# Sliding-window attention feeding a token mixer on one core: the token matrix reassociated away, and the score matmuls of two heads interleaved

## The chip, the cores and the metric

The kernel runs on one core of one Trainium2 chip. The metric is device time in microseconds, from start to end of one execution. The profile's span (first to last instruction) is about 2 us shorter. PE is the matrix engine, DVE the vector engine, ACT the scalar engine, POOL the engine that issues the loads. All ratios below are computed as the mean time of one kernel's fast runs over the mean of the fast runs of the other kernel in the same rounds, so they are not quite the ratios of the medians that are quoted.

## The reference, cut to what matters

```python
# q, k, v: (8 batches, 8 heads, 576 positions, 64)
scores = where(0 <= i-j < 128, q @ k.T / 8 - slope[h] * |i-j|, -1e9)
attn   = softmax(scores) @ v                       # per batch and head
x      = attn.transpose(0, 2, 1, 3).reshape(8, 576, 512)
# token mixing, per batch; w_q and w_k are (512, 64)
wq = x @ w_q                                       # 576 x 64
wk = x @ w_k                                       # 576 x 64
W_tok = wq @ wk.T / 8                              # 576 x 576, nothing nonlinear on it
mixed = W_tok @ x                                  # 576 x 512
out   = relu(mixed) @ w_out
```

## The kernel before: the parts that the change and the argument touch

The program is unrolled. The attention of batch b and the token mixing of batch b-1 are cut into chunks and laid down alternately; a scheduler then orders each engine's instructions. Two PSUM buffers of 1,024 fp32 columns (`pscore`) hold scores, four buffers of up to 512 (`ppool`) serve everything else.

```python
        def mk_qk(h):                       # scores of one head, five key blocks
            def f():
                ...
                ps = pscore.tile([P, 1024], FP32, name=f"ps{h}", tag="ps")
                for kb in range(NKB):
                    o, w = KB_OFF[kb], KB_WID[kb]
                    nc.tensor.matmul(ps[:, o : o + w],
                        kT[hb : hb + 64, hp, 128 * kb : 128 * kb + 128],   # 64 rows
                        qT[hb : hb + 64, hp, 128 * kb : 128 * kb + w], start=True, stop=True)
                pt = spool.tile([P, 1024], F16, name=f"pt{h}", tag="pt", bufs=8)
                nc.scalar.activation(out=pt, in_=ps, func=AF.Exp, scale=SCALE)
                nc.vector.tensor_tensor(out=pt, in0=pt, in1=bfull[h], op=ALU.mult)
...
        def mk_wtok(tcn):                   # 128 rows of the token matrix
            def f():
                ...
                nc.tensor.matmul(pw, lt, wqkT[0][:, 0:512], start=True, stop=True)
                nc.tensor.matmul(pwl, lt, wqkT[0][:, 512:576], start=True, stop=True)
                cp(nc.vector, dst[:n, 0:512], pw[:n])
                cp(nc.vector, dst[:n, 512:], pwl[:n])
...
        def mk_mixed(db):                   # 128 of 512 channels of the mixed result
            def f():
                ...
                for tcn in range(NQT):      # five contraction tiles, each a pair of matmuls
                    nc.tensor.matmul(pm, lt, st_["wtok"][tcn][:n, 0:512], ...)
                    nc.tensor.matmul(pml, lt, st_["wtok"][tcn][:n, 512:], ...)
                nc.scalar.activation(out=rm[:, db, 0:512], in_=pm, func=AF.Relu, scale=WSCALE)
                nc.scalar.activation(out=rm[:, db, 512:], in_=pml, func=AF.Relu, scale=WSCALE)
...
        chunks = [[mk_wq(0)], [mk_wtok(0), mk_wtok(1), mk_wtok(2)], [mk_wtok(3), mk_wtok(4)]]
        for db in range(4):
            chunks.append([mk_mixed(db)])
        for st in range(NQT):
            chunks.append([mk_out(st)])
```

The softmax here doesn't subtract the row's maximum and nothing guards it: scores larger than these inputs give would overflow.

## Time and profile before

The median is 270.46 us (270.09 to 270.84, two runs); the profiled run has a span of 267.9 us. I cut the span by events that can be found on the engine timelines. A period begins with a batch's first transposing matmul (tile `ptr`). Its part A ends where the batch's first exponential starts on ACT, part B ends with the eighth bias multiplication on DVE, part C ends where the next period begins. The last period ends with the first projection matmul (tile `pw`) of the last batch. What lies ahead of batch 1's period is the start, what follows the last period is the tail.

| before, us | start | A | B | C | period (mean of 7) | tail |
|---|---|---|---|---|---|---|
| length | 36.3 | 6.01 | 12.55 | 11.32 | 29.89 | 22.4 |
| of it at half clock | all | 0.7 | 4.9 | 0.5 | 6.1 | 8.1 |

The first two fences are from the profile page of before: the busy table, and the row of the 40-slice table that has the PE clock granted, in tenths.

```profile
PE 227.3 (85%) x2000; PEld 130.1 (49%) x2000; DVE 164.4 (61%) x426; ACT 128.9 (48%) x234; POOL 108.2 (40%) x134
...
PEclk9999999799968999879979997799959998899689
```

No engine is full, and the clock dips once in every period. The clock records begin at 41.4 us; ahead of that the row prints full clock because there is no record. There 128-column matmuls follow each other after 0.107 us, against 0.056 us at recorded full clock, so I count the start as half clock; the 0.7 us in A is the first part of batch 1's period. The mean clocks that the profile gives (0.915 here) count the start as full.

This is the stretch view of before for batch 4: parts A, B and C. The columns are the stretch, its length, then busy us of each engine with instruction counts, the granted clock, and DMA.

```profile
core 0: us, PE busy (x) PEld busy (x) DVE busy (x) ACT busy (x) POOL busy (x), PEclk, DMA share, GB/s
128.20:133.90 5.70, 5.00 (x62) 3.57 (x61) 3.16 (x7) 3.90 (x10) 5.70 (x8) 1.00 1.90 177
133.90:146.50 12.60, 10.28 (x77) 5.30 (x76) 8.38 (x20) 10.20 (x17) 5.14 (x7) 0.86 1.45 93
146.50:157.60 11.10, 10.89 (x116) 6.50 (x115) 8.83 (x28) 0.85 (x3) 1.71 (x2) 1.00 0.20 73
```

In part B, ACT is the engine with the most to do, but it is not back to back. This is the ACT timeline of before in that part; a bracket gives idle time just before the instruction and who ended it.

```profile
136.77 1.02 ACT L153 ACTIVATE pt_1975<-ps_1969 128x1024 f16<-128x1024 f32 x1
137.97 1.02 ACT L153 ACTIVATE pt_1999<-ps_1993 128x1024 f16<-128x1024 f32 x1 [0.18 <-PE ps_1993 L146]
...
140.81 0.60 ACT L270 ACTIVATE rm<-pm 128x512 f16<-128x512 f32 x1 [1.68 <-PE pml L268]
141.31 0.22 ACT L271 ACTIVATE rm<-pml 128x64 f16<-128x64 f32 x1
141.41 1.03 ACT L153 ACTIVATE pt_2008<-ps_2002 128x1024 f16<-128x1024 f32 x1
```

Between the fifth and the sixth exponential ACT stands 1.68 us for the first mixing pass. The PE and DVE timelines of before:

```profile
138.83 0.61 PE L266 MATMUL pm<-wtok_1914,x_1629 128*128 128x512 f16 x1
139.24 0.26 PE L268 MATMUL pml<-wtok_1914,x_1629 128*128 128x64 f16 x1
139.31 0.61 PE L266 MATMUL pm<-wtok_1921,x_1669 128*128 128x512 f16 x1
...
140.99 0.38 PE L266 MATMUL pm<-wtok_1914,x_1629 128*128 128x512 f16 x1
```

```profile
133.33 0.69 DVE L51 CAST wtok_1907<-pwt 128x512 f16<-128x512 f32 x1
133.94 0.21 DVE L51 CAST wtok_1907<-pwtl 128x64 f16<-128x64 f32 x1
134.07 0.68 DVE L51 CAST wtok_1914<-pwt 128x512 f16<-128x512 f32 x1
134.67 0.21 DVE L51 CAST wtok_1914<-pwtl 128x64 f16<-128x64 f32 x1
134.80 0.68 DVE L51 CAST wtok_1921<-pwt 128x512 f16<-128x512 f32 x1
```

From 136.9 to 140.4 the clock records say half clock, and a mixing pair takes 0.48 us from start to start (138.83 to 139.31) against 0.25 us at full clock. The records of matmuls overlap (0.38 us long, 0.25 us from pair to pair), so distances between starts are what adds up.

### The profile page before, as it was taken

What the parts mean: (1) busy time and instruction counts of PE and PEld (TensorE: products, weight loads), DVE (VectorE), ACT (ScalarE), POOL (GpSimd) and SP (SyncE); (2) the same over time, 40 slices, a digit from 0 to 9 for tenths busy, and PEclk for the clock granted to TensorE, in tenths of its full rate; (3) what the DMA queues carried; (4) which work ended last, traced back from release to release, by engine and by line L of the source; (5) the groups of instructions that cost most, each with busy time, mean ns of one, the idle gap of its engine ahead of it and who ended that gap; (6) DMA issues with size and microseconds to landing.
All of it is one profiled execution on the core that took longest, in us unless ns stands there. A gap on an engine that the chain in (4) does not pass through costs nothing.

```text
span 267.9 us, 5117 instructions
## 1 busy us (share of the span) xinstructions
PE 227.3 (85%) x2000; PEld 130.1 (49%) x2000; DVE 164.4 (61%) x426; ACT 128.9 (48%) x234; POOL 108.2 (40%) x134
## 2 busy tenths in 40 slices
PE   0477798989899997979888997989899998998894
PEld 0244665445544654445644655455544654454331
DVE  1134837578674858368594858477674869485504
ACT  3977218640767139540577128640767048711130
POOL 9999859402960079001970079102950000000000
PEclk9999999799968999879979997799959998899689
DMA  4999999903990299903992289903990220013005
GB/s 30 111 140 133 155 100 134 114 4 118 170 152 4 81 134 159 72 1 120 152 155 19 81 120 164 80 0 125 177 145 1 87 92 2 0 46 123 11 1 177
DMA packets 120425, 24.72 MB, mean 92 GB/s; under 512 B 115280, under 2 KB 115792, under 8 KB 120400
## 3 DMA queue, kind: packets, MB, share of 16 engines
q0 software_dynamic: 115152, 14.95, 86.9%
q1 hardware_dynamic: 5248, 9.44, 9.8%
q8 instruction: 15, 0.25, 0.4%
q14 instruction: 10, 0.08, 0.1%
HBM read 29.88 MB, written 9.44 MB: 147 GB/s over the span
## 4 chain that ended last, share of the span: by engine, by line
PE 35%; ACT 16%; issue 16%; DMA 13%; POOL 11%; DVE 8%; POOLq 0%; ACTq 0%
PE pm L266 12%; PE po L281 7%; DMA vnat<-in_v_dram 5%; PE px L180 4%; ACT rm L270 3%; POOL vnat L116 3%; DMA knat_433<-in_k_dram 3%; DVE osb L51 2%; DMA knat_3179<-in_k_dram 2%; DMA knat_126<-in_k_dram 2%; PE pml L268 1%; DMA qnat_886<-in_q_dram 1%; PE pxt L199 1%; ACT qT L49 1%; PE ptr L133 1%
## 5 line engine op out<-in xcount | busy, mean ns | idle before, releaser
L116 POOL DMA_DIRECT2D vnat<-in_v_dram x40 | 34.4, 884 | 85.6 <-issue 66.6
L49 ACT COPY qT<-ptr 128x512 f16<-128x512 f16 (+1 forms) x24 | 12.5, 521 | 70.5 <-PE ptr L133 70.3
L281 PE MATMUL po<-wout_sb,rm 128*128 128x512 f16 x160 | 41.2, 384 | 1.0
L51 DVE COPY osb<-po 128x512 f32<-128x512 f32 (+1 forms) x40 | 27.5, 688 | 12.9 <-PE po L281 11.9
L270 ACT ACTIVATE rm<-pm 128x512 f16<-128x512 f32 x32 | 19.6, 614 | 32.0 <-PE pml L268 32.0
L146 PEld LDWEIGHTS <-kT 64*128 64x128 f16 x320 | 25.2, 103 | 17.2 <-issue 9.2
L183 DVE RECIPROCAL invr<-px 128x4 f32<-128x4 f32 (+1 forms) x80 | 12.5, 171 | 17.1 <-PE px L180 17.0
L51 DVE COPY kT<-ptr 128x512 f16<-128x512 f16 (+1 forms) x24 | 9.1, 380 | 21.5 <-PE ptr L133 21.3
L281 PEld LDWEIGHTS <-rm 128*128 128x128 f16 x160 | 14.4, 99 | 14.2 <-issue 3.5
L51 DVE COPY xT<-pxt 128x512 f16<-128x512 f16 (+1 forms) x40 | 15.5, 388 | 0.7 <-PE pxt L199 0.5
L49 ACT COPY kT<-ptr 128x512 f16<-128x512 f16 x16 | 9.4, 588 | 3.8 <-PE ptr L133 3.8
L51 DVE COPY qT<-ptr 128x512 f16<-128x512 f16 x16 | 6.7, 421 | 5.2 <-PE ptr L133 5.2
L229 PE MATMUL pw<-xT,wqk_sb 128*128 128x512 f16 x32 | 9.9, 410 | 0.0
L271 ACT ACTIVATE rm<-pml 128x64 f16<-128x64 f32 x32 | 7.3, 230 | 0.0
L231 PE MATMUL pwl<-xT,wqk_sb 128*128 128x64 f16 x32 | 6.3, 201 | 0.0
L49 ACT CAST wqkT_3636<-pw 64x512 f16<-64x512 f32 x1 | 0.6, 580 | 10.2 <-PE pwl L231 10.2
L133 PE MATMUL ptr<-identh,qnat_108 128*128 128x128 f16 x4 | 0.6, 308 | 5.7 <-DMA qnat_108<-in_q_dram 5.7
L54 ACT ACTIVATE vnat<-identh 128x45 f16<-128x45 f16 x8 | 3.3, 412 | 3.5 <-DMA vnat<-in_v_dram 3.3
L229 PEld LDWEIGHTS <-wqk_sb 128*128 128x128 f16 x32 | 3.3, 104 | 3.3 <-issue 0.8
L249 PE MATMUL pwt<-wqkT_3636,wqkT_3637 64*128 64x512 f16 x5 | 2.2, 460 | 2.3 <-ACT wqkT_3637 L49 1.3
L54 ACT ACTIVATE kT<-bfull_88 128x256 f16<-128x256 f16 x8 | 3.6, 453 | 0.0
L231 PEld LDWEIGHTS <-wqk_sb 128*128 128x128 f16 x32 | 3.2, 103 | 0.2
(1015 smaller groups left out, 717.3 us busy)
## 6 DMA issues: line engine op xcount, KB each, us to landing
out_dram<-osb SPq DMA_DIRECT2D x32, 256.0 KB, 2.0
vnat<-in_v_dram POOLq DMA_DIRECT2D x32, 128.0 KB, 5.1
out_dram<-osb SPq DMA_DIRECT2D x8, 128.0 KB, 4.0
vnat<-in_v_dram POOLq DMA_DIRECT2D x8, 64.0 KB, 4.8
wout_sb<-in_moe_w_out_dram POOLq DMA_DIRECT2D x1, 512.0 KB, 6.4
qnat_108<-in_q_dram POOLq DMA_DIRECT2D x1, 128.0 KB, 3.5
knat_110<-in_k_dram POOLq DMA_DIRECT2D x1, 128.0 KB, 3.4
qnat_112<-in_q_dram POOLq DMA_DIRECT2D x1, 128.0 KB, 3.3
```

The lines of the kernel that those rows point to most:

```text
L49: eng.copy(out_ap, in_ap)
L51: eng.tensor_copy(out=out_ap, in_=in_ap)
L116: nc.gpsimd.dma_start(out=vnat[:n, kt, 0:H, 1:65], in_=v[b, :, ss, :].transpose([1, 0, 2]))
L146: nc.tensor.matmul(ps[:, o : o + w], kT[hb : hb + 64, hp, 128 * kb : 128 * kb + 128], qT[hb : hb + 64, hp, 128 * kb : 128 * kb + w], start ...
L180: nc.tensor.matmul(px[:, hh, :], lt, rt, start=(i == 0), stop=(i == len(mms) - 1))
L183: nc.vector.reciprocal(out=invr[:n], in_=px[:n, :, 0])
L229: nc.tensor.matmul(pw, wqk_sb[:, dc, :], xT[:, dc, 0:512], start=(dc == 0), stop=(dc == 3))
L231: nc.tensor.matmul(pwl, wqk_sb[:, dc, :], xT[:, dc, 512:576], start=(dc == 0), stop=(dc == 3))
L266: nc.tensor.matmul(pm, lt, st_["wtok"][tcn][:n, 0:512], start=(tcn == 0), stop=(tcn == 4))
L270: nc.scalar.activation(out=rm[:, db, 0:512], in_=pm, func=AF.Relu, scale=WSCALE)
L271: nc.scalar.activation(out=rm[:, db, 512:], in_=pml, func=AF.Relu, scale=WSCALE)
L281: nc.tensor.matmul(po, rm[:, db, lo : lo + 128], wout_sb[:, db, :], start=(db == 0), stop=(db == 3))
```

## The change

The intent: (wq wk^T) x equals wq (wk^T x). The product in brackets, G, is 64 x 512 and takes five matmuls; the 576 x 576 matrix, its ten copies out of PSUM per batch, and 16 of 20 pairs of mixing matmuls go away. wk is now needed with positions on rows, which takes 20 narrow matmuls. The second idea: the heads of a pair lie on rows 0 to 63 and 64 to 127, so their score matmuls are issued alternately, meant to run side by side.

```diff
-        def mk_qk(h):
+        def mk_qk2(hp):
...
+                pss = [pscore.tile([P, 1024], FP32, name=f"ps{hp}_{i}", tag="ps") for i in range(2)]
                 for kb in range(NKB):
                     o, w = KB_OFF[kb], KB_WID[kb]
-                    nc.tensor.matmul(ps[:, o : o + w], kT[hb : hb + 64, ...], qT[hb : hb + 64, ...])
+                    for i in range(2):
+                        hb = 64 * i
+                        nc.tensor.matmul(pss[i][:, o : o + w], kT[hb : hb + 64, ...], qT[hb : hb + 64, ...])
...
-        def mk_wtok(tcn): ...                       # five token tiles, ten copies
+        def wk():                                   # wk with positions on rows
+            for t in range(NQT):
+                for dc in range(4):
+                    nc.tensor.matmul(pk[:n, t, :], xT[:, dc, 128 * t : 128 * t + n],
+                                     wqk_sb[:, dc, 64:128], start=(dc == 0), stop=(dc == 3))
+            cp(nc.vector, wkn[:, 0:4, :], pk[:, 0:4, :])
+            cp(nc.vector, wkn[:64, 4, :], pk[:64, 4, :])
+        def gmat():                                 # G = wk^T x, 64 x 512
+            for t in range(NQT):
+                nc.tensor.matmul(pg[0:64], st_["wkn"][:n, t, :], ast["xs"][t][:n, :], ...)
+            cp(nc.scalar, g, pg[0:64])
         def mk_mixed(db):
-                for tcn in range(NQT): ...          # five pairs of matmuls
+                lt = st_["g"][:, 128 * db : 128 * db + 128]        # 64 rows
+                nc.tensor.matmul(pm, lt, st_["wqT"][:, 0:512], start=True, stop=True)
+                nc.tensor.matmul(pml, lt, st_["wqT"][:, 512:576], start=True, stop=True)
```

Cut from the diff: two fewer weight loads, two fewer copies and one fewer zero fill on ACT in the projection, and second buffers for `rm`, `wqT` and the new tiles.

More of the change, by code (lines that the diff above doesn't have):

```diff
@@ L87 @@
     wqk_sb = cpool.tile([P, 4, 128], F16, name="wqk_sb")
-    wkq_sb = cpool.tile([P, 4, 128], F16, name="wkq_sb")
     wout_sb = cpool.tile([P, 4, DM], F16, name="wout_sb")
     def load_weights():
-        for src, dsts in ((moe_w_q, (wqk_sb[:, :, 0:64], wkq_sb[:, :, 64:128])),
-                          (moe_w_k, (wqk_sb[:, :, 64:128], wkq_sb[:, :, 0:64]))):
-            for dst in dsts:
-                nc.gpsimd.dma_start(out=dst, in_=src.rearrange("(c p) j -> p c j", p=P))
+        for src, dst in ((moe_w_q, wqk_sb[:, :, 0:64]), (moe_w_k, wqk_sb[:, :, 64:128])):
+            nc.gpsimd.dma_start(out=dst, in_=src.rearrange("(c p) j -> p c j", p=P))
         nc.gpsimd.dma_start(out=wout_sb, in_=moe_w_out.rearrange("(c p) j -> p c j", p=P))
@@ L136, in mk_xpose @@
             return f
-        def mk_qk(h):
+        def mk_qk2(hp):
             def f():
                 qT, kT = st_["qT"], st_["kT"]
-                hp = h // 2
-                hb = (h % 2) * 64
-                ps = pscore.tile([P, 1024], FP32, name=f"ps{h}", tag="ps")
+                pss = [pscore.tile([P, 1024], FP32, name=f"ps{hp}_{i}", tag="ps") for i in range(2)]
                 for kb in range(NKB):
                     o, w = KB_OFF[kb], KB_WID[kb]
-                    nc.tensor.matmul(
-                        ps[:, o : o + w],
-                        kT[hb : hb + 64, hp, 128 * kb : 128 * kb + 128],
-                        qT[hb : hb + 64, hp, 128 * kb : 128 * kb + w],
-                        start=True, stop=True,
-                    )
-                pt = spool.tile([P, 1024], F16, name=f"pt{h}", tag="pt", bufs=8)
-                nc.scalar.activation(out=pt, in_=ps, func=AF.Exp, scale=SCALE)
-                nc.vector.tensor_tensor(out=pt, in0=pt, in1=bfull[h], op=ALU.mult)
-                st_.setdefault("pts", {})[h] = pt
+                    for i in range(2):
+                        hb = 64 * i
+                        nc.tensor.matmul(
+                            pss[i][:, o : o + w],
+                            kT[hb : hb + 64, hp, 128 * kb : 128 * kb + 128],
+                            qT[hb : hb + 64, hp, 128 * kb : 128 * kb + w],
+                            start=True, stop=True,
+                        )
+                for i in range(2):
+                    h = 2 * hp + i
+                    pt = spool.tile([P, 1024], F16, name=f"pt{h}", tag="pt", bufs=8)
+                    nc.scalar.activation(out=pt, in_=pss[i], func=AF.Exp, scale=SCALE)
+                    nc.vector.tensor_tensor(out=pt, in0=pt, in1=bfull[h], op=ALU.mult)
+                    st_.setdefault("pts", {})[h] = pt
             return f
@@ L208, in attn_chunks @@
         for h in range(0, H, 2):
-            chunks.append([mk_qk(h), mk_qk(h + 1)])
+            chunks.append([mk_qk2(h // 2)])
         for qt in range(NQT):
@@ L219, in moe_chunks, with wq @@
         st_ = {}
-        def mk_wq(_):
-            def f():
-                xT = ast["xT"]
-                d0 = spool.tile([64, 640], F16, name="wqkT0", tag="wqkT0", bufs=1)
-                d1 = spool.tile([64, 640], F16, name="wqkT1", tag="wqkT1", bufs=1)
-                pw = ppool.tile([P, DM], FP32, name="pw", tag="p1")
-                pwl = ppool.tile([P, DH], FP32, name="pwl", tag="p1")
+        def wq():
+            xT = ast["xT"]
+            d0 = spool.tile([64, S], F16, name="wqT", tag="wqT", bufs=2)
+            pw = ppool.tile([P, DM], FP32, name="pw", tag="p1")
+            pwl = ppool.tile([P, DH], FP32, name="pwl", tag="p1")
+            for dc in range(4):
+                nc.tensor.matmul(pw[0:64], wqk_sb[:, dc, 0:64], xT[:, dc, 0:512],
+                                 start=(dc == 0), stop=(dc == 3))
+                nc.tensor.matmul(pwl[0:64], wqk_sb[:, dc, 0:64], xT[:, dc, 512:576],
+                                 start=(dc == 0), stop=(dc == 3))
+            cp(nc.scalar, d0[:, 0:512], pw[0:64])
+            cp(nc.scalar, d0[:, 512:576], pwl[0:64])
+            st_["wqT"] = d0
@@ L228, in f @@
+        def wk():
+            xT = ast["xT"]
+            pk = ppool.tile([P, NQT, DH], FP32, name="pk", tag="p1")
+            for t in range(NQT):
+                n = QT_N[t]
                 for dc in range(4):
-                    nc.tensor.matmul(pw, wqk_sb[:, dc, :], xT[:, dc, 0:512],
+                    nc.tensor.matmul(pk[:n, t, :], xT[:, dc, 128 * t : 128 * t + n],
+                                     wqk_sb[:, dc, 64:128],
                                      start=(dc == 0), stop=(dc == 3))
-                    nc.tensor.matmul(pwl, wqk_sb[:, dc, :], xT[:, dc, 512:576],
-                                     start=(dc == 0), stop=(dc == 3))
@@ L233, in f @@
-                cp(nc.scalar, d0[:, 0:512], pw[0:64])
-                cp(nc.scalar, d0[:, 512:576], pwl[0:64])
-                cp(nc.scalar, d1[:, 0:512], pw[64:128])
-                cp(nc.scalar, d1[:, 512:576], pwl[64:128])
-                fill(d1[:, 576:640], 0.0, identh[0:64, 0:64])
-                st_["wqkT"] = {0: d0, 1: d1}
-            return f
-        def mk_wtok(tcn):
-            def f():
-                wqkT = st_["wqkT"]
-                n = QT_N[tcn]
-                dst = spool.tile([P, S], F16, name=f"wtok{tcn}", tag=f"wtok{tcn}", bufs=1)
-                pw = ppool.tile([P, DM], FP32, name="pwt", tag="p1")
-                pwl = ppool.tile([P, DH], FP32, name="pwtl", tag="p1")
-                lt = wqkT[1][:, 128 * tcn : 128 * tcn + 128]
-                nc.tensor.matmul(pw, lt, wqkT[0][:, 0:512], start=True, stop=True)
-                nc.tensor.matmul(pwl, lt, wqkT[0][:, 512:576], start=True, stop=True)
-                cp(nc.vector, dst[:n, 0:512], pw[:n])
-                cp(nc.vector, dst[:n, 512:], pwl[:n])
-                st_.setdefault("wtok", {})[tcn] = dst
-            return f
+            wkn = spool.tile([P, NQT, DH], F16, name="wkn", tag="wkn", bufs=2)
@@ new lines, in wk @@
+            cp(nc.vector, wkn[:, 0:4, :], pk[:, 0:4, :])
+            cp(nc.vector, wkn[:64, 4, :], pk[:64, 4, :])
+            st_["wkn"] = wkn
+        def gmat():
+            pg = ppool.tile([P, DM], FP32, name="pg", tag="p1")
+            for t in range(NQT):
+                n = QT_N[t]
+                nc.tensor.matmul(pg[0:64], st_["wkn"][:n, t, :], ast["xs"][t][:n, :],
+                                 start=(t == 0), stop=(t == NQT - 1))
+            g = spool.tile([64, DM], F16, name="gm", tag="gm", bufs=2)
+            cp(nc.scalar, g, pg[0:64])
+            st_["g"] = g
@@ L258, in f @@
                 if db == 0:
-                    st_["rm"] = spool.tile([P, 4, S], F16, name="rm", tag="rm", bufs=1)
+                    st_["rm"] = spool.tile([P, 4, S], F16, name="rm", tag="rm", bufs=2)
                 rm = st_["rm"]
@@ L262, in f @@
                 pml = ppool.tile([P, DH], FP32, name="pml", tag="p1")
-                for tcn in range(NQT):
-                    n = QT_N[tcn]
-                    lt = ast["xs"][tcn][:n, 128 * db : 128 * db + 128]
-                    nc.tensor.matmul(pm, lt, st_["wtok"][tcn][:n, 0:512],
-                                     start=(tcn == 0), stop=(tcn == 4))
-                    nc.tensor.matmul(pml, lt, st_["wtok"][tcn][:n, 512:],
-                                     start=(tcn == 0), stop=(tcn == 4))
+                lt = st_["g"][:, 128 * db : 128 * db + 128]
+                nc.tensor.matmul(pm, lt, st_["wqT"][:, 0:512], start=True, stop=True)
+                nc.tensor.matmul(pml, lt, st_["wqT"][:, 512:576], start=True, stop=True)
                 nc.scalar.activation(out=rm[:, db, 0:512], in_=pm, func=AF.Relu, scale=WSCALE)
@@ L288, in mk_out @@
             return f
-        chunks = [[mk_wq(0)], [mk_wtok(0), mk_wtok(1), mk_wtok(2)],
-                  [mk_wtok(3), mk_wtok(4)]]
+        chunks = [[wq], [wk], [gmat]]
         for db in range(4):
```

## The prediction

> **What bounds it now.** The span is 267.9 us (page header) against a measured 270.46. From the first transposes of each batch on the PE timeline, it splits into a start (36.3 us, batch 0's attention, loads and cold clock), seven steady periods (36.3 to 245.5, 29.9 us each: attention of batch b beside token mixing of b-1) and a tail (22.4 us, mixing of the last batch alone). No engine is full in a period: the window 128.6 to 158.0 has PE 26.2, DVE 20.3, ACT 15.0 us busy of 29.4. Loads are not the limit: the queries and keys of the next batch issue from 130 to 138, land about 5 us later, and are first used at 157.6.
>
> A period has three parts, from the engine timelines:
> - A, 5.3 us, transposes and projections; ACT evacuates nearly without gaps.
> - B, about 12.4 us, scores and exponentials: eight exponentials at about 0.92 us pitch on ACT, with ACT waiting 1.7 us once and 0.5 us for mixing matmuls, because PE is at half clock from 136.9 to 140.4 and a mixing pass of 5 pairs takes 2.4 us there against 1.3 at full clock.
> - C, about 11.7 us, attention times V, output: mostly DVE bound, 1.81 us per query tile; the last mixing pass (1.4 us) delays its start.
>
> **What the change does, per batch.**
> - Removes the token matrix: 5 matmul pairs (about 0.25 us each), ten DVE copies (0.61+0.13 each pair in pitch, 3.7 us in all), two ACT copies and a zero fill (0.8 us).
> - Mixing shrinks from 20 matmul pairs to 4 (0.25 us each warm): about 4 us less PE warm, more cold.
> - Adds 20 narrow matmuls for wk (0.03 to 0.06 us pitch, as the PV matmuls: 0.6 to 1.2 us), two small DVE copies (0.3), five G matmuls (0.22 each, 1.1), one ACT copy of G (0.5).
> - Score interleaving: the built program interleaves two heads only for the first pair of a batch; the other three pairs stand as five and five, as before. I give it nothing.
>
> **On the critical path.** A: minus 0.7 (ACT copies), plus 0.3 (wk ahead of the scores). B: ACT's waits for cold mixing vanish, one G copy is added; the relus stay: minus 1.5 to 2. C: the last mixing pass shrinks by about 1 us, partly given back[...]: cold stretches of 3.4 or 6.8 us every period, 512-column pitch 0.43 against 0.22. I expect 3.4 us more cold per period, costing about 1 us in C. Net about 2.5 us per period, period 27.4; seven give 17. Tail: token-matrix copies (3 us) and mixing (8 us) become about 5.5: minus 5.5. Start: two small weight loads fewer, 0 to 1.
>
> Total about 23 us: predicted **247 us**, 8 in 10 within **239 to 257**. Chances: faster by over 2% 0.95, within 2% 0.04, slower 0.01.
>
> **What would show it.** Period 26.3 to 28.5; tail 16 to 18; DVE busy per period about 17; ACT about the same; B near 10.5 with ACT back to back; C still about 1.8 per query tile; lower mean clock (about 0.88); PE busy well below 85%.
>
> **What would make it wrong.** If the clock stays cold through C (PE needs over 3 us per query tile there), most of the gain is lost: 255 or more. If the new chain wk, copy, G, copy, mixing delays the score matmuls behind it in PE's order, B does not shrink. If the clock stays warm, the period falls to 25.5 and the time towards 235.

About 17 us from seven periods, 5.5 from the tail and 0 to 1 from the start come to about 23 us. The 3.4 us more at half clock, costing about 1 us in C, are my estimate: one more of the 3.4 us stretches that the clock records of before show.

## The result, and the profile after

The changed kernel took 248.53 us (248.46 to 248.6); its ratio to before is 0.921 (95% interval 0.911 to 0.931). A later run of three rounds on another chip gave 246.85 us (245.65 to 248.34) and 0.914. In the profiled run the span is 246.7 us.

| us | start | A | B | C | period | tail |
|---|---|---|---|---|---|---|
| before | 36.3 | 6.01 | 12.55 | 11.32 | 29.89 | 22.4 |
| changed | 36.0 | 5.97 | 9.91 | 11.78 | 27.67 | 17.0 |
| half clock, before | all | 0.7 | 4.9 | 0.5 | 6.1 | 8.1 |
| half clock, changed | all | 0.8 | 5.3 | 5.0 | 11.1 | 3.4 |

Seven periods give 15.5 us, the tail 5.4, the start 0.3. All of the period's gain is in B; A hardly moved and C became longer. These are the busy table and the clock row of the changed kernel's page:

```profile
PE 211.7 (86%) x1864; PEld 128.1 (52%) x1864; DVE 142.0 (58%) x362; ACT 121.5 (49%) x218; POOL 106.6 (43%) x132
...
PEclk9999999957996599857995599858995699759979
```

The stretch view of the changed kernel, parts A, B and C of batch 4:

```profile
120.30:126.00 5.70, 5.38 (x79) 3.82 (x77) 3.02 (x8) 3.22 (x8) 5.70 (x8) 1.00 1.87 176
126.00:135.90 9.90, 8.27 (x53) 4.48 (x53) 6.08 (x11) 9.90 (x16) 5.22 (x7) 0.73 1.86 119
135.90:147.70 11.80, 11.73 (x106) 7.20 (x104) 8.50 (x27) 0.82 (x4) 1.73 (x2) 0.79 0.18 67
```

In B, ACT is now busy for 9.90 of 9.90 us: the eight exponentials, one copy of G and the evictions of the mixing passes stand back to back, as its timeline shows (no brackets):

```profile
130.67 1.04 ACT L152 ACTIVATE pt_1870<-ps_0_1858 128x1024 f16<-128x1024 f32 x1
131.58 1.04 ACT L152 ACTIVATE pt_1873<-ps_1_1859 128x1024 f16<-128x1024 f32 x1
132.48 0.62 ACT L268 ACTIVATE rm<-pm 128x512 f16<-128x512 f32 x1
```

PE looks as busy as before (86% against 85%) with 136 fewer matmuls, because more of its work is done at half clock: the mean recorded clock fell from 0.915 to 0.848. The cost is visible in C. This is the PE timeline of the changed kernel there: the output projection of one query tile at half clock, halfway, and at full clock.

```profile
137.24 1.91 PE L279 MATMUL po<-wout_sb,rm 128*128 128x512 f16 x4
...
140.26 1.33 PE L279 MATMUL po<-wout_sb,rm 128*128 128x512 f16 x4
...
142.36 1.02 PE L279 MATMUL po<-wout_sb,rm 128*128 128x512 f16 x4
```

In every period from the second on, the clock records have the same pattern: 10.24 us at half and 17.07 at full, together 27.31 us, which is also the period, to within 0.1 us, six times in a row. The records change state only at multiples of 3.413 us.

### The profile page after: what moved, and what is told of

It is laid out like the page before. It is cut to its first block, busy times and chain, and to the rows that moved or that the text cites. A ratio compares the mean times of both kernels' runs of the same rounds, so it can differ in the third digit from the quotient of the medians.

```text
span 246.7 us, 4766 instructions
## 1 busy us (share of the span) xinstructions
PE 211.7 (86%) x1864; PEld 128.1 (52%) x1864; DVE 142.0 (58%) x362; ACT 121.5 (49%) x218; POOL 106.6 (43%) x132
## 4 chain that ended last, share of the span: by engine, by line
PE 65%; ACT 13%; DVE 7%; POOL 6%; issue 6%; DMA 2%; ACTq 0%; POOLq 0%
PE po L279 19%; PE px L179 15%; PE ptr L130 7%; PE pxt L198 5%; PE pw L226 4%; PE pk L240 3%; ACT rm L268 2%; DVE osb L51 2%; PE pm L266 2%; DMA vnat<-in_v_dram 2%; ACT qT L49 1%; POOL vnat L113 1%; ACT gm L49 1%; DVE invr L182 1%; PE pg L252 1%
## 5 line engine op out<-in xcount | busy, mean ns | idle before, releaser
L279 PE MATMUL po<-wout_sb,rm 128*128 128x512 f16 x160 | 50.4, 451 | 0.7 <-ACT rm L268 0.2
L143 PEld LDWEIGHTS <-kT 64*128 64x128 f16 x320 | 27.4, 106 | 25.5 <-issue 17.7
L279 PEld LDWEIGHTS <-rm 128*128 128x128 f16 x160 | 17.1, 116 | 17.3 <-issue 10.1
L51 DVE COPY kT<-ptr 128x512 f16<-128x512 f16 (+1 forms) x24 | 9.1, 381 | 20.0 <-PE ptr L130 18.8
L266 PE MATMUL pm<-wqT,gm 64*128 64x512 f16 x32 | 14.1, 474 | 5.8 <-ACT gm L49 0.7
L51 DVE COPY xT<-pxt 128x512 f16<-128x512 f16 (+1 forms) x40 | 15.5, 388 | 1.0 <-PE pxt L198 0.5
L49 ACT CAST wqT<-pw 64x512 f16<-64x512 f32 x8 | 4.6, 579 | 16.8 <-PE pwl L228 16.8
L226 PE MATMUL pw<-xT,wqk_sb 128*64 128x512 f16 x32 | 10.1, 416 | 0.0
L51 DVE CAST wkn<-pk 128x256 f16<-128x256 f32 (+1 forms) x16 | 4.4, 315 | 5.6 <-PE pk L240 5.6
L252 PEld LDWEIGHTS <-wkn 128*64 128x64 f16 (+1 forms) x40 | 3.7, 108 | 7.4 <-issue 3.3
L266 PEld LDWEIGHTS <-gm 64*128 64x128 f16 x32 | 3.0, 95 | 8.0 <-ACT gm L49 1.0
L240 PE MATMUL pk<-wqk_sb,xT 128*128 128x64 f16 (+1 forms) x160 | 7.1, 195 | 0.0
L267 PE MATMUL pml<-wqT,gm 64*128 64x64 f16 x32 | 6.7, 208 | 0.0
L240 PEld LDWEIGHTS <-xT 128*128 128x128 f16 (+1 forms) x160 | 5.8, 100 | 1.5 <-issue 0.2
```

The lines of the kernel that those rows point to most:

```text
L49: eng.copy(out_ap, in_ap)
L51: eng.tensor_copy(out=out_ap, in_=in_ap)
L143: nc.tensor.matmul(pss[i][:, o : o + w], kT[hb : hb + 64, hp, 128 * kb : 128 * kb + 128], qT[hb : hb + 64, hp, 128 * kb : 128 * kb + w], s ...
L226: nc.tensor.matmul(pw[0:64], wqk_sb[:, dc, 0:64], xT[:, dc, 0:512], start=(dc == 0), stop=(dc == 3))
L240: nc.tensor.matmul(pk[:n, t, :], xT[:, dc, 128 * t : 128 * t + n], wqk_sb[:, dc, 64:128], start=(dc == 0), stop=(dc == 3))
L266: nc.tensor.matmul(pm, lt, st_["wqT"][:, 0:512], start=True, stop=True)
```

## The experiments

Theory at the outset: the reassociation is the whole gain; B shrank because 16 mixing pairs fewer stand between the exponentials; the interleave does nothing; less PE work costs clock in C (the estimate above, not shown at that point). Rivals: the interleave contributes; the ten DVE copies, not the matmuls, were what stretched B. Twelve kernels ran. All results were correct except the one that is wrong on purpose. Parts are means over seven periods of the profiled run; "half" is the time at half clock in B and C.

| run | median us | ratio to before | A | B | C | half B / C | period | tail |
|---|---|---|---|---|---|---|---|---|
| e1_assoc_only | 246.27 | 0.913 | 5.69 | 9.90 | 11.63 | 4.7 / 4.6 | 27.21 | 17.0 |
| after_again | 246.85 | 0.914 | 5.77 | 9.88 | 11.57 | 4.3 / 4.4 | 27.21 | 16.9 |
| e2_pair_only | 273.94 | 1.012 | 6.12 | 12.96 | 11.70 | 4.2 / 2.2 | 30.78 | 21.6 |
| e3_scores_twice | 289.43 | 1.075 | 6.26 | 14.83 | 11.85 | 7.1 / 5.1 | 32.94 | 18.1 |
| e4_mix_five | 257.15 | 0.944 | 5.85 | 10.02 | 12.58 | 0 / 4.4 | 28.45 | 23.1 |
| e5_few_copies | 247.32 | 0.917 | 6.22 | 10.09 | 10.78 | 0 / 0 | 27.09 | 18.1 |
| e6_dead_token | 263.46 | 0.976 | 6.50 | 11.79 | 11.35 | 4.9 / 3.8 | 29.63 | 17.2 |
| e7_fill128 | 244.66 | 0.905 | 5.83 | 10.21 | 10.56 | 0 / 0 | 26.60 | 18.5 |
| e8_fill64 | 255.31 | 0.940 | 5.77 | 10.13 | 12.37 | 1.7 / 4.1 | 28.27 | 18.8 |
| e9_fill_inner | 239.42 | 0.886 | 5.85 | 10.21 | 10.46 | 0 / 0 | 26.53 | 16.8 |
| e10_all | 260.48 | none | 7.42 | 12.31 | 10.21 | see text | 29.94 | 18.6 |
| e11_pv128 | 227.40 | 0.844 | 5.64 | 10.21 | 9.02 | 0 / 0 | 24.87 | 17.8 |

The profiled runs of e2, e4, e8 and e10 were slow ones of their kernels (1.5% or more above the fastest). The parts of these four are used only for what the clock records of the same profile say, and not against fast runs where a few tenths matter. The record calls the comparisons of e2, e6 and e11 with before unclear; for e11 four of before's seven runs counted as slow, so three are left to compare with.

### The two parts of the change, one at a time

e1_assoc_only keeps the reassociation and goes back to head-by-head scores; e2_pair_only is the kernel before with only the interleave; after_again is the changed kernel once more.

```diff
 # e1, on the changed kernel; e2 is the reverse edit on the kernel before
-            chunks.append([mk_qk2(h // 2)])
+            chunks.append([mk_qk(h), mk_qk(h + 1)])
```

Expected of e1_assoc_only:

> The changed kernel with the score matmuls written head by head as before; the reassociated mixing stays. Theory (all of the gain is the reassociation, the interleave is inert because in the changed kernel only the first pair of a batch stands interleaved on PE): the same as the changed kernel, 248.5 us plus or minus 1.5, and a period of 27.3 us. Rival (the interleave of the first pair shortens the way to the first exponential and the ten matmuls side by side count): 0.3 to 1 us per batch longer, 251 to 257 us.

Expected of e2_pair_only:

> The kernel before with only the score matmuls of two heads interleaved; the 576x576 token matrix stays. Theory: within 1% of before, 268 to 273 us, with the period near 29.9 us and the same half-clock stretches of 3.4 or 6.8 us. Rival (the interleave is worth something by itself): 262 to 267 us, with the stretch from the first transposes to the first exponential shorter than 5.7 us.

Expected of after_again:

> The changed kernel once more, beside the runs of before on this chip, to see whether its 248.5 us and the 246.3 us of the version without the interleave differ by more than chips and runs do. Expected 247 to 249 us; if the interleave costs nothing, its runs will spread down to 246.

e1 gave 0.913 (0.905 to 0.921) and after_again 0.914 (0.908 to 0.920): within the noise, the reassociation is the whole gain. e2 gave 1.012 (1.001 to 1.022), if anything a loss. Part of the reason is in the order on PE: in the built changed kernel only the first pair of a batch stands alternately, as the start times of its first scores show; the other three pairs stand five and five, because the second buffer of a pair comes free only after its own exponential (in batch 4, PE waits 0.26 to 0.38 us for an exponential ahead of three of the later heads) and the scheduler does not let the first head wait. The steady A of e1 is 5.55 us against 5.63, so where the interleave does happen it costs 0.08 us: the first exponential then waits for nine or ten matmuls and not for five.

### Was it PE's thin work in B that cost the clock?

e3_scores_twice issues every score matmul twice into the same place.

```diff
-                        nc.tensor.matmul(pss[i][:, o : o + w], ...)
+                        for _ in range(2):
+                            nc.tensor.matmul(pss[i][:, o : o + w], ...)
```

> The changed kernel with each score matmul issued twice into the same place (the same result, 40 more matmuls per batch, nothing else). Theory that the half clock in the later part of each batch is the price of a PE with little to do between exponentials: PE is then busy nearly all of an exponential's 0.92 us pitch, the granted clock stays at 1.0 for longer (half-clock stretch below 7 us per period instead of 10.2), the output part falls from 11.8 towards 10.5 us and the time falls or stays: 238 to 249 us, although work was added. Rival (the clock falls anyway, or PE is the limit there): at half clock two heads then need about 4 us against 1.84 us of exponentials, the score part grows from 9.9 to 14 us or more and the time is 265 to 290 us.

The rival was right: 289 us, and more half clock, not less. Work was added and the clock still fell (mean 0.834 against 0.848). That was the first sign that not every busy PE microsecond counts alike.

### Mixing matmuls or copies?

e4_mix_five gives PE as many mixing pairs as before but no token matrix.

```diff
-                nc.tensor.matmul(pm, lt, st_["wqT"][:, 0:512], start=True, stop=True)
-                nc.tensor.matmul(pml, lt, st_["wqT"][:, 512:576], start=True, stop=True)
+                for _ in range(5):
+                    nc.tensor.matmul(pm, lt, st_["wqT"][:, 0:512], start=True, stop=True)
+                    nc.tensor.matmul(pml, lt, st_["wqT"][:, 512:576], start=True, stop=True)
```

> The changed kernel with each pair of mixing matmuls issued five times, so that PE has as many mixing matmuls as before, while the token matrix, its ten vector-engine copies and its matmuls stay away. Theory (the score part shrank because the exponentials no longer stand behind mixing matmuls run at half clock): the score part goes back from 9.9 towards 12 us, the start of the output part is delayed by about 1 us, period 29 to 30 us, 260 to 270 us. Rival (the ten copies on the vector engine were the cost): the score part stays below 10.5 us and the time within 2% of 248.5 us, 246 to 253.

B stayed at 10.02 us in each of the seven periods, all at full clock. The profiled run was a slow one, but a B that is wholly at full clock was not lengthened by the clock. Its stretch view for part B of batch 4 has ACT full:

```profile
127.60:137.60 10.00, 8.84 (x77) 4.92 (x77) 6.08 (x12) 10.00 (x17) 5.26 (x7) 1.00 1.91 122
```

So the theory fell here, as far as full clock goes: 20 mixing pairs between the exponentials do not by themselves stretch B. What 20 pairs at half clock would do without the copies, e4 does not show. The time rose all the same (fast runs 254.3 and 254.7 us, slow ones 259.6 and 260.4), outside both expectations. In the profiled run 6 us of it are the tail, where the added pairs stand alone, and the rest is C; the fast runs have no profile.

e5_few_copies goes the other way: the kernel before, every matmul kept, but only 64 of 576 columns of each token tile are copied out of PSUM. The tiles otherwise hold a constant, and the result is wrong.

```diff
-                dst = spool.tile([P, S], F16, name=f"wtok{tcn}", tag=f"wtok{tcn}", bufs=1)
+                dst = wtoks[tcn]            # standing tiles, filled once with 0.01
...
-                cp(nc.vector, dst[:n, 0:512], pw[:n])
-                cp(nc.vector, dst[:n, 512:], pwl[:n])
+                cp(nc.vector, dst[:n, 0:64], pw[:n, 0:64])
```

> The kernel before, all matmuls kept, but of each token-matrix tile only 64 of 576 columns are copied out of PSUM (the rest of the tile holds a constant; the result is wrong on purpose). That takes about 3 us per batch of vector-engine copies away, and the waits of the token matmuls for a free PSUM buffer behind them. Theory (those copies spaced the matmuls out, the thin stretch let the clock fall to half, and the mixing matmuls at half clock held up the exponentials): the score part falls from 12.55 to 10 to 11 us though all 20 mixing pairs are still there, period near 28 us, 252 to 260 us. Rival (the 20 mixing pairs themselves are the cost): score part above 12 us, 264 us or more.

It took 247.32 us, ratio 0.917 (0.911 to 0.923): the time of the changed kernel, with all 2,000 matmuls of before. This is its stretch view, parts A, B and C of batch 4:

```profile
119.50:125.50 6.00, 5.30 (x66) 3.77 (x65) 3.15 (x9) 3.90 (x9) 6.00 (x8) 1.00 1.86 172
125.50:135.60 10.10, 9.16 (x77) 4.93 (x74) 6.58 (x13) 10.02 (x17) 4.92 (x7) 1.00 1.77 114
135.60:146.40 10.80, 10.60 (x114) 6.39 (x112) 8.54 (x28) 0.71 (x2) 1.69 (x2) 1.00 0.20 75
```

PE's instruction counts are those of before (66, 77 and 114 against 62, 77 and 116); ACT is full in B, and the clock is 1.00 throughout. The copies are not removed without side effects: the scheduler, seeing short copies, also lays the mixing pairs between the scores instead of in one block after them. So what is shown is that shortening the copies, with all that it does to PSUM buffers, order and clock, brings the whole gain, and that the count of matmuls need not fall for it. Buffers, order and clock are not separated.

e6_dead_token is the counter-check: the changed kernel with a token matrix computed again and thrown away, five pairs and ten copies per batch in the old places.

```diff
-        chunks = [[wq], [wk], [gmat]]
+        chunks = [[wq], [wk, mk_dead(0), mk_dead(1), mk_dead(2)], [gmat, mk_dead(3), mk_dead(4)]]
```

> The changed kernel with a token matrix computed again beside it and thrown away: five matmul pairs and ten vector-engine copies per batch at the places where they stood before; mixing stays at four pairs. Theory (copies and their buffers are what stretched the score part): it goes from 9.9 to 11.3 us or more, 257 to 268 us. Rival (they fit into idle time once the mixing pairs are gone): the score part stays below 10.6 us, 248 to 253 us.

It took 263.46 us, ratio 0.976 (0.970 to 0.982), with B at 11.79 us in every period: 1.9 of the 2.6 us that the change had gained there came back. The edit adds five matmul pairs as well as copies, so alone it would not separate them; e5, which keeps the five token pairs and has B at 10.09 us, does. But the wait is not the one of before. In each of the seven periods ACT stands twice in B, 0.75 us for the matmuls of G and 0.87 us for the next scores, both at full clock:

```profile
135.59 0.58 ACT L49 CAST gm<-pg 64x512 f16<-64x512 f32 x1 [0.75 <-PE pg L252]
137.04 1.94 ACT L152 ACTIVATE pt<-ps 128x1024 f16<-128x1024 f32 x2 [0.87 <-PE ps L143]
```

So here the token matrix costs time in B without the clock. That PE was held up by buffers that the copies keep is likely (a dead pair waits 0.28 us for a DVE copy just before), and not shown.

### What the clock follows

The clock records, e10's apart, have two states, 1.0 and 0.5, and the changes lie multiples of 3.413 us apart. Idle PE stretches do not explain the half clock: the longest in batch 4 of the changed kernel is 0.63 us, and the clock fell all the same.

So I cut the traces of before, the changed kernel and all experiments but e10 into windows of 3.413 us at the times where the records can change, counted the columns of the matmuls that start in each, and compared with the clock in the next window. (Back to back, 512-column matmuls start 0.216 us apart at full clock, nearly 16 in a window; I take 16 times 512, about 8,190 columns, as a full one. This fill is an estimate from that.) In the seven periods of these 13 runs there are 588 windows at full clock, of which 66 were followed by half clock:

| fill of the window, at full clock | followed by half clock | followed by full clock |
|---|---|---|
| columns alone | 0.12 to 0.76 | 0.42 to 1.04 |
| columns times active rows / 128 | 0.12 to 0.38 | 0.35 to 0.89 |

With columns alone the two groups overlap widely. With rows counted, they part at about 0.37, with nine windows in the overlap (four, if a matmul that runs over the end of a window is split between the two). Transposes count here like other matmuls: without them the overlap grows to 160. The time in which any matmul streams, an obvious rival, does not part the groups either: its best line misplaces 58 of the 588. A score matmul uses 64 of 128 rows and would then count half; so do the changed kernel's mixing pairs (contraction over 64), where the mixing pairs of before had 128 rows. That would be why e3 failed and why the changed kernel loses clock: the window of batch 4 from 127.2 us is filled to 0.63 by columns but 0.32 by rows. The way back has the same line: of the 151 windows at half clock those that stayed there have 0.05 to 0.43 in these columns times rows, those followed by full clock 0.36 to 0.53 (half clock can stream about 0.5, an estimate from the 0.427 us between its 512-column matmuls in before and the changed kernel, against 0.216). One line at 0.37 is right for 730 of the 739 windows in both states.

This was found by fitting, so e7_fill128 tests it: filler matmuls over 128 rows, written where the next real matmul overwrites them. e8_fill64 uses the same places and the same columns with 64 rows.

```diff
+    def filler(ap, w):                       # e7; e8 takes 64 rows of the same operands
+        nc.tensor.matmul(ap, bfull[0][:, 0:128], bfull[0][:, 0:w], start=True, stop=True)
...
+                for i in range(2):           # ahead of each pair of heads
+                    filler(pss[i][:, 0:512], 512)
+                    filler(pss[i][:, 512:768], 256)
```

The cut parts: two fillers of 256 columns in each half of the first query tile, two of 512 ahead of the last mixing pair.

> The changed kernel with filler matmuls over all 128 rows of the array that write where the next real matmul overwrites them: 512 and 256 columns ahead of each head's scores, and four of 256 and two of 512 columns around the first query tile (about 8,200 columns per batch, 3.4 us of PE at full clock; the result is unchanged). In the traces so far, a 3.4 us window at full clock was followed by half clock whenever columns times active rows filled at most 0.36 of the array, and by full clock from 0.37 on; a score matmul uses 64 rows and counts half. Theory: the fillers lift the score part above that line, the clock stays at 1.0 in it and in the output part, which falls from 11.8 to about 10.5 us; score part 9.9 to 10.3; period 26 to 26.5 us; 236 to 242 us although work was added. Rival (the clock follows time or gaps, not rows, or the fillers delay the scores): half clock remains, PE is the limit, 250 us or more.

> The run with fillers once more, same places, same columns, so the same PE time, but each filler uses 64 rows of the array instead of 128. Theory (the clock follows columns times active rows): the score part stays below the line of 0.36 per window (about 0.28), the clock falls to half there as in the changed kernel or longer, granted clock below 0.90, and since the extra work is then done at half clock, the score part grows beyond 11 us: 255 to 280 us. Rival (any PE work counts alike): as with 128 rows, granted clock 0.98, 243 to 246 us.

e7 took 244.66 us (ratio 0.905, 0.900 to 0.911) with the clock at 1.0 through B and C of every period; its stretch view for batch 4:

```profile
118.40:124.00 5.60, 5.31 (x79) 3.79 (x77) 2.99 (x8) 3.20 (x7) 5.60 (x8) 1.00 1.83 177
124.00:134.20 10.20, 9.38 (x69) 4.59 (x69) 5.96 (x12) 10.13 (x17) 5.27 (x7) 1.00 1.85 117
134.20:144.70 10.50, 10.36 (x110) 6.33 (x110) 8.39 (x28) 0.96 (x4) 1.72 (x2) 1.00 0.21 77
```

B costs 0.3 us more, C 1.2 us less than in the changed kernel (C 10.56 against 11.78). The period was as expected, but the total missed the expected 236 to 242 because the fillers lengthened the half-clock start by about 2 us and the tail by 1.5. e8, the same columns on 64 rows, took 255.31 us (fast runs 252.4 and 254.1) with a granted clock of 0.93 and 0.94 in the fast runs against 0.98. The same columns at half the rows do not hold the clock, which is what counting rows says; the rival is excluded. My expectation for e8 was too dark, though (clock below 0.90, B beyond 11 us; B is 10.13): the second window in B came out at 0.33 to 0.38 in three batches, where the clock fell within B, and at 0.39 to 0.41 in the other four, where it held there and in three of them fell at the passage to C.

e9_fill_inner drops the fillers in batch 0 and in the tail.

```diff
-                for i in range(2):
+                for i in range(2 if b > 0 else 0):
```

> The 128-row fillers only where they paid: not in the first batch, which ran at half clock anyway and grew by 1.7 us there, and not in the tail (the mixing of the last batch alone), which grew by 1.5 us. Expected: steady period 26.3 us as with all fillers, start near 36.4, tail near 17: 240 to 243 us. If the start or the tail were slow for another reason, 244 to 246.

As expected, and a little better: 239.42 us, ratio 0.886 (0.881 to 0.892), on the same chip as e8; steady periods of 26.29 us, tail 16.8.

### Going on

e10_all added two edits to e9: two of four mixing evictions moved to DVE, and the last key tile of attention times V padded with zero rows from 64 to 128.

```diff
+            nc.gpsimd.memset(vnat[64:128, 4, :, :], 0.0)
...
-                    if qt == 4:
-                        mms.append((pts[h][0:64, o : o + 128], vnat[:64, qt, h, 0:65]))
+                    mms.append((pts[h][:, o : o + 128], vnat[:, qt, h, 0:65]))
...
+                if db < 2: ...              # for both parts of the tile
+                    nc.vector.tensor_scalar(out=rm[:, db, lo:hi], in0=p, scalar1=WSCALE,
+                                                   scalar2=0.0, op0=ALU.mult, op1=ALU.max)
```

> The run before with two more edits: the first two of four mixing evictions per batch go from the scalar engine, which is back to back in the score part, to the vector engine, which has gaps there (0.58 us each off the chain of exponentials); and the last key tile of attention times V is padded with zero rows to 128, so that its 16 matmuls, which alternate between 128 and 64 rows and take 2.15 us against 0.5 us for the other query tiles at full clock, are all of 128 rows. Expected: score part 10.2 to about 9.1, output part 10.5 to about 9, period near 23.7 us, 220 to 228 us. If the vector engine becomes the limit or the clock falls again for lack of work, 230 us or more.

It failed: 260.48 us (254.08 to 265.88), three of four runs slow, and the one fast run (254.08) is also far from the expected 220 to 228. Two causes can be read in the profiled run, a slow one. The split fill of V's ones on ACT landed between two transposes' copies and waited 2.49 us there; the fourth load of V landed 0.14 us before it started. And from 34.7 us on, the clock records of the profiled run have a third state, 0.752, with half-clock stretches in between, as its clock row shows:

```profile
PEclk9999987777777777777655677677767777777767
```

What set that state is open. e11_pv128 does only the padding, on e9, with two standing V tiles whose ones and zero rows are written once.

```diff
-            vnat = spool.tile([P, NQT, H + 1, 1 + D], F16, name="vnat", tag="vnat", bufs=2)
+            vnat = vnats[b % 2]
...
-            fill(vnat[:, :, :, 0], 1.0, identh[:, 0 : NQT * (H + 1)])
```

> The kernel with inner fillers (239.4 us) with one of the two edits of the run before, done so that nothing else is added: two standing tiles for V, whose ones and zero rows are written once, and the last key tile of attention times V taken with 128 rows, so that PE no longer alternates between 128-row and 64-row matmuls there. Theory (the alternation itself costs 2.15 against 0.5 us, and the vector engine waits 0.3 and 0.9 us for it): output part 10.45 to between 8.9 and 9.4, score part 10.2 as before, period about 25, clock above 0.97, 226 to 232 us. Rivals: the vector engine takes up the gain and the output part stays above 9.9, 235 us or more; or the granted clock falls to about 0.75 again as in the run before, 240 us or more, which would tie that state to this edit.

It took 227.40 us, ratio 0.844 (0.832 to 0.856), the fastest version, with a clock of 0.985; so the padding does not bring the third state by itself. The PE timelines show its effect. First e9, then e11: 16 matmuls of one query tile, the last one in e9 alternating between 128 and 64 rows.

```profile
137.01 0.65 PE L189 MATMUL px<-vnat,pt 128*128 128x65 f16 x16
...
138.82 2.22 PE L189 MATMUL px<-vnat,pt 128*128 128x65 f16 x16
```

```profile
128.25 0.65 PE L192 MATMUL px<-vnat,pt 128*128 128x65 f16 x16
...
130.07 0.65 PE L192 MATMUL px<-vnat,pt 128*128 128x65 f16 x16
```

The 16 matmuls took 2.22 us alternating between 128 and 64 rows and 0.65 us at 128 rows throughout, and C fell from 10.46 to 9.02 us; why alternating takes longer, the trace does not show. The time is 5% below e9's 239.42 us, on another chip. The standing V tiles also took one fill per batch off ACT; C's change is nearly that of PE's last tile (1.57 us). About 10 of the 13.6 us between the two profiled spans lie in C; the start is 2.9 us shorter too, where the fill of V's ones no longer holds PE up (1.86 us in e9) and full clock comes at 28.4 us and not at 34.3.

## Why the prediction was right, and where it was not

The time (247 predicted, 248.5 measured, range 239 to 257), the period (27.4, measured 27.67) and the tail (minus 5.5, measured minus 5.4) were right. Point by point:

- **Score interleaving, "I give it nothing": right.** e1 and after_again have the same ratio, and e2 gains nothing.
- **Part A, minus 0.7 plus 0.3: too much.** Measured minus 0.04 (steady periods 5.74 to 5.63). The ACT copies are gone, but on PE 20 wk matmuls (0.8 us) stand ahead of most of the first scores.
- **Part B, "ACT's waits for cold mixing vanish": the effect was right, its size was not, and its cause only in part.** Minus 2.64 was measured against minus 1.5 to 2. The prediction had the waits end because mixing shrinks from 20 pairs to 4. e4 has the 20 pairs back and B stays at 10.0; e5 keeps every matmul of before and has B at 10.1; e6 keeps mixing at 4 pairs, puts token pairs and copies back, and has B at 11.8: 0.8 of the 2.6 us is left. The mis-sized term is the ten DVE copies, which I listed as removed work (3.7 us on DVE) and gave no place on the critical path; DVE was only 69% busy in the period (20.3 of 29.4 us). How they cost B is argued. In before the window from 133.5 us has only 64-row matmuls, scores and token pairs, and is filled to 0.30 with rows counted; then the clock fell, and the 128-row mixing pairs, which need the copies, came at half clock. In e5 they come into these windows, which have about 0.46 and 0.53. In e6, though, B is stretched at full clock. No run held the clock in the kernel before with its copies kept, which would tell the two apart. And of the two waits that the prediction gave to mixing, the trace puts the second (0.53 us) down to a load of V.
- **Part C, minus 1 "partly given back": more than given back.** With the clock held, C is 10.46 us (e9), so about 0.9 of the minus 1 was there; at half clock it is 11.78. The clock thus takes 1.3 us per period where I had put about 1, and half clock grew from 6.1 to 11.1 us per period (10.2 in the steady ones) where I had put 3.4 us more.
- **Tail, right in sum.** It now runs at half clock for 3.4 us instead of 8.1, which I had not counted.
- **"PE busy well below 85%": wrong**, 86%. Busy time stretches when the clock falls (a mixing pair takes 0.48 us at half clock and 0.25 at full), so it is no measure of work removed. DVE busy 17.6 us per steady period (predicted 17), ACT back to back in B, and a lower mean clock (0.848; predicted 0.88) came as said.

The errors cancelled: B gained more and A and C less than written. That the period came within 0.3 us is luck to that extent.

One thing stays half open. The steady period of the changed kernel equals eight clock windows (27.31 us). In after_again, where the phase began differently, five successive periods were 26.74, 27.01, 27.19, 27.25 and 27.28 us while the half clock in C grew from 4.0 to 4.9 us and C from 11.33 to 11.73. e1, whose A is 0.08 us shorter, drifts to the same period. With the clock held, the period is 26.29 us, no multiple of the window. It looks as if a period shorter than eight windows makes the half-clock stretch slide later into C until the gain is eaten. No run forced the phase, so this is argued and not shown.

## What to carry to other kernels

Removing work from PE can lower its clock, and then the stage after it pays: here 136 fewer matmuls came with a mean clock of 0.848 instead of 0.915, and C took 11.78 us against 10.46 with the clock held (e9). Before counting matmuls saved, look at the clock row and ask how many array rows the remaining matmuls use; here the clock fell after windows filled to at most 0.38 with rows counted. An engine that is only 60 to 70% busy can still be the cause, as when the busiest chain needs its copies to be done: test it by cutting the copies and keeping the matmuls (B went from 12.55 to 10.09 us in e5). And a padding to full rows that seems to waste half the array can be cheaper than the half-row matmul, here by 1.4 us per batch.
